# Scores of five batches from unpadded, DMA-transposed q in two bursts a batch, and the tails of two batches in one channel product

## The chip, the cores and the metric

The kernel runs on one core of one Trainium2 chip, as one launch. The metric is its device time in microseconds. The engines are named as the profile names them: PE (TensorE, matmuls) with its weight loads PEld, DVE (VectorE), ACT (ScalarE), POOL (GpSimd) and SP (SyncE), which issues most of the DMAs.

## What is computed

A windowed attention feeds an MLP mixer. Batch 8, 8 heads, 576 positions, head size 64; the model width is 512. Heads 0 to 3 ("plain") see the last 32 positions, heads 4 to 7 ("dilated") every fourth of the last 128. Cut to what matters:

```python
scores = matmul(q, k.transpose(0, 1, 3, 2)) / sqrt(D)        # D = 64
rel = pos[:, None] - pos[None, :]
mask_plain = (rel >= 0) & (rel < 32)                         # heads 0..3
mask_dil = (rel >= 0) & (rel < 128) & (rel % 4 == 0)         # heads 4..7
attn = softmax(where(mask, scores, -1e9))
x = matmul(attn, v)  as  [B, 576, 512]
h = relu(x.T @ w_tok1) @ w_tok2                              # tokens: 576 -> 256 -> 576
u = x + h.T
out = u + relu(u @ w_ch1) @ w_ch2                            # channels: 512 -> 1536 -> 512
```

## The kernel before, in words

All products run in float16 with float32 sums in PSUM. A batch passes through these stages, and the batches overlap: while batch b is in its channel product, batch b+1 passes through values and token mixing, and the scores of b+2 are made.

*Layout.* The 576 positions are four blocks of 128 and a tail of 64. Heads go in pairs, `hp` 0 and 1 plain, 2 and 3 dilated; a pair's 2 x 64 head dimensions fill the 128 partitions. The 512 main positions of a dilated head are held by their remainder modulo 4 (r) and their quotient (m), so that a residue's 128 positions form one dense block under the plain band mask of 32.

*Scores.* `score` (L401) makes one block, transposed, with the keys on the output's partitions: the stationary operand is 128 keys of a pair, both heads' dimensions on the 128 rows, and the moving operand is `qz`, which holds q of one head on its 64 rows and zeros on the other 64. So a matmul contracts over 128 rows, of which half are zeros. `scores_plain` (L415) takes three blocks of 128 keys by 160 queries a head, then in a small bank the fourth block of 160 and the tail of 64; `scores_dil` (L445) takes four residues of 128 by 128 a head, then two tail blocks of 64. ACT takes the exp of each bank (L426, L435, L438, L455, L463) into `attp` and `attd`; in batches 2 and up POOL multiplies these by the band and tail masks (L113 by `mult`). In batches 0 and 1 a further matmul adds a "veil" of large negative numbers instead.

*q and k.* They are loaded, cast by POOL (`c_q`, `c_k`, L103), and turned over: in batches 0 to 2 by PE transposes, from batch 3 on by DMA transposes on SP (`dma_steps`, L346) into `qt`, `kr` (by residue) and `tt` (the tails). `place_steps` (L361) then copies these into `qz` and `kt`: POOL (L371, L373) brings the plain pairs into natural order, DVE (L367, L368, L377, L382) the tails and the dilated pairs.

*Values and mixing.* `values` (L471) multiplies with v; a column of ones gives the sums, and DVE divides (L501, L113). `emit_h1` and `emit_u` are the token mixing. u is turned over by PE (`emit_uT`, L541) up to batch 2 and by DMA from batch 3 on (`uT_dma`, L567; two of its four channel blocks are brought into natural order by ACT into `utd`, `uT_place`, L582).

*Channel product.* `gen_main` (L624) is the long stream: 12 blocks `gp` of four matmuls of 512 columns (L645), each followed by a relu on ACT or DVE (L107, L109); after blocks 5 and 8, `gp_tails` (L632) does the 64 tail columns of this batch, 6 blocks at a time (L636). Then come the token blocks `yp` (L664), 2 x 12 matmuls of 256 columns each, whose result DVE adds to u and SP stores. Two batches, an even and the following odd one, share one token block for their tails (`yp`, L684, in the odd batch).

*The order* is written out by hand: each engine executes its instructions in the order of emission. `interleave` (L693) emits `gen_main`, which says at each step what it costs in microseconds, and a list of side steps, each with a place (the time from the batch's start at which it is due) and a cost; a side step is emitted as soon as the sum of costs reaches its place. "Place 16.2" below means such a due time. It binds no clock; it fixes the order in every engine's queue, SP's included. In batch b from 2 on (L894 and following): values of b+1 from 0.4, casts of b+2 from 2.0, mixing of b+1 from 5.4, DMA transposes of b+2 from 8.5, placements from 13.0 (POOL) and 15.5 (DVE), loads of b+3 from 13.0, scores of b+2 from 16.2 with 2.7 between the pairs (the scores of a pair one spacing later than that), and the placement of u at 29.2.

*PSUM* has eight banks: three `main` (used in rotation by the channel product), two `sc` (rotation) and three `fl` (values and mixing).

## Time and profile before

| | us |
|---|---|
| median of 3 runs | 296.73 (296.33 to 298.97) |
| the profiled execution | 296.67 |
| its span, first to last instruction | 294.9 |
| granted TensorE clock, mean | 0.998 of full speed |
| DMA: moved, mean rate | 52.36 MB, 178 GB/s |

The prediction shows the lines. A line of the timeline has start, duration, engine, line of the kernel, operation, out<-in by the program's names, shape and count; consecutive instructions of a kind are merged (x6), and a bracket gives idle time ahead and what ended it. A PE shape "128\*128 128x160" means 128 rows contracted, 128 stationary columns, 160 moving columns. The recorded duration of a matmul holds its latency and overlaps the next one's. A group of instructions shows count, busy us, mean ns of one, and idle time ahead of them with what ended it.

### The profile page before, as it was taken

What the parts mean: (1) busy time and instruction counts of PE and PEld (TensorE: products, weight loads), DVE (VectorE), ACT (ScalarE), POOL (GpSimd) and SP (SyncE); (2) the same over time, 40 slices, a digit from 0 to 9 for tenths busy, and PEclk for the clock granted to TensorE, in tenths of its full rate; (3) what the DMA queues carried; (4) which work ended last, traced back from release to release, by engine and by line L of the source; (5) the groups of instructions that cost most, each with busy time, mean ns of one, the idle gap of its engine ahead of it and who ended that gap; (6) DMA issues with size and microseconds to landing.
All of it is one profiled execution on the core that took longest, in us unless ns stands there. A gap on an engine that the chain in (4) does not pass through costs nothing.

```text
span 294.9 us, 7473 instructions
## 1 busy us (share of the span) xinstructions
PE 283.1 (96%) x3010; PEld 221.1 (75%) x3010; DVE 153.7 (52%) x326; ACT 132.5 (45%) x259; POOL 181.5 (62%) x246
## 2 busy tenths in 40 slices
PE   5799999999999999999999999999999999999995
PEld 2686679986767977698776977797767977796584
DVE  5775438856738965722744165723753265423122
ACT  2864336376552534356344634365345624323400
POOL 6992056439999899749992999369993920000000
PEclk9999999999999999999999999999999999999999
DMA  7999999987996999699779988499936220421023
GB/s 213 272 213 178 209 322 216 335 189 212 275 190 132 270 288 162 170 210 295 182 106 284 240 216 159 119 293 263 156 66 110 74 71 2 85 81 67 2 71 108
DMA packets 104562, 52.36 MB, mean 178 GB/s; under 512 B 72880, under 2 KB 103472, under 8 KB 104528
## 3 DMA queue, kind: packets, MB, share of 16 engines
q1 hardware_dynamic: 100288, 46.81, 66.9%
q0 software_dynamic: 2640, 3.91, 7.6%
q10 hardware_dynamic: 1600, 1.18, 1.3%
q8 instruction: 23, 0.38, 0.5%
q14 instruction: 11, 0.09, 0.1%
HBM read 37.04 MB, written 9.44 MB: 158 GB/s over the span
## 4 chain that ended last, share of the span: by engine, by line
PE 83%; DMA 6%; POOL 4%; ACT 2%; DVE 2%; SPq 1%; issue 1%; ACTq 0%; POOLq 0%
PE gp L645 27%; PE yp L664 26%; PE gt L636 4%; PE h1p L512 4%; PE up L524 4%; PE sc L406 4%; PE yp L684 4%; DMA w<-in_moe_w_ch_dram 3%; DMA l_q<-in_q_dram 2%; ACT utd L582 1%; PE sm L406 1%; PE av L493 1%; PE h1p L510 1%; PE av L482 1%; PE up L535 1%; DMA l_vt<-in_v_dram 1%
## 5 line engine op out<-in xcount | busy, mean ns | idle before, releaser
L664 PE MATMUL yp<-w,gt 128*128 128x256 f16 x756 | 93.3, 273 | 0.7 <-DVE gt L109 0.7
L664 PEld LDWEIGHTS <-gt 128*128 128x128 f16 x768 | 76.5, 106 | 5.6 <-issue 0.9
L107 ACT ACTIVATE gt<-gp 128x512 f16<-128x512 f32 x69 | 41.2, 597 | 71.4 <-PE gp L645 71.1
L645 PEld LDWEIGHTS <-w 128*128 128x128 f16 x384 | 39.2, 114 | 22.8 <-issue 2.1
L113 POOL TENSOR_TENSOR attp<-attp,const 128x1280 f16<-128x1280 f16 (+1 forms) x24 | 36.4, 1544 | 28.7 <-ACT attp L435 28.5
L674 DVE TENSOR_TENSOR o<-yp,u 128x512 f32<-128x512 f32 x31 | 21.3, 690 | 58.3 <-PE yp L664 55.3
L645 PE MATMUL gp<-utd,w 128*128 128x512 f16 x120 | 45.6, 380 | 0.6 <-ACT utd L582 0.4
L645 PE MATMUL gp<-utm,w 128*128 128x512 f16 x120 | 45.5, 379 | 0.0
L645 PE MATMUL gp<-uT,w 128*128 128x512 f16 x144 | 37.2, 379 | 0.5 <-DMA w<-in_moe_w_ch_dram 0.3
L113 POOL TENSOR_TENSOR attd<-attd,const 128x1024 f16<-128x1024 f16 (+1 forms) x24 | 32.8, 1402 | 0.0
L113 DVE TENSOR_TENSOR xn<-av,rec 128x320 f16<-128x320 f32 x64 | 31.5, 492 | 2.2
L109 DVE TENSOR_SCALAR gt<-gp 128x512 f16<-128x512 f32 x27 | 18.6, 687 | 17.4 <-PE gp L645 16.5
L406 PEld LDWEIGHTS <-kt 128*128 128x128 f16 x272 | 22.4, 101 | 3.5 <-DVE kt L315 1.4
L426 ACT ACTIVATE attp<-sc 128x480 f16<-128x480 f32 x32 | 17.8, 572 | 12.1 <-PE sc L406 12.0
L373 POOL COPY qz<-qt 64x512 f16<-64x512 f16 x20 | 21.6, 1081 | 0.6
L530 DVE TENSOR_TENSOR u<-up,xn 128x512 f16<-128x512 f32 x26 | 17.4, 689 | 8.3 <-PE up L524 8.1
L103 POOL CAST c_q<-l_q 128x512 f16<-128x512 f32 x31 | 19.1, 620 | 4.2 <-DMA l_q<-in_q_dram 4.2
L107 ACT ACTIVATE h<-h1p 128x256 f16<-128x256 f32 x29 | 11.1, 384 | 21.9 <-PE h1p L512 21.9
L103 POOL CAST c_k<-l_k 128x512 f16<-128x512 f32 x29 | 17.9, 620 | 4.2 <-DMA l_k<-in_k_dram 2.8
L455 ACT ACTIVATE attd<-sc 128x512 f16<-128x512 f32 x32 | 18.7, 596 | 4.1 <-PE sc L406 3.6
L501 DVE RECIPROCAL rec<-av 128x5 f32<-128x5 f32 x64 | 12.2, 190 | 13.3 <-PE av L488 6.7
L406 PE MATMUL sc<-qz,kt 128*128 128x160 f16 (+1 forms) x144 | 18.1, 228 | 1.0 <-DVE kt L315 1.0
(138 smaller groups left out, 484.5 us busy)
## 6 DMA issues: line engine op xcount, KB each, us to landing
out_dram<-o SPq DMA_DIRECT2D x72, 128.0 KB, 3.1
l_q<-in_q_dram SPq DMA_DIRECT2D x15, 512.0 KB, 6.1
l_k<-in_k_dram SPq DMA_DIRECT2D x14, 512.0 KB, 5.7
l_vn<-in_v_dram SPq DMA_DIRECT2D x32, 128.0 KB, 5.8
l_vd<-in_v_dram SPq DMA_DIRECT2D x16, 256.0 KB, 4.2
w<-in_moe_w_ch_dram POOLq DMA_DIRECT2D x6, 512.0 KB, 7.7
lt<-in_q_dram SPq DMA_DIRECT2D x8, 128.0 KB, 3.9
l_vt<-in_v_dram SPq DMA_DIRECT2D x8, 128.0 KB, 4.7
```

The costliest lines, as they stand in the source:

```text
L103: eng.tensor_copy(out=out, in_=in_)
L107: nc.scalar.activation(out=out, in_=in_, func=AF.Relu)
L109: eng.tensor_scalar_max(out=out, in0=in_, scalar1=0.0)
L113: eng.tensor_tensor(out=out, in0=x, in1=y, op=ALU.mult)
L373: nc.gpsimd.tensor_copy(out=natural(qz[hp][halves[h], h, 0:512]), in_=qta[halves[h], hp].rearrange("p r m -> p m r"))
L406: nc.tensor.matmul(out=out, lhsT=lhsT, rhs=qz[hp][:, h, queries], start=hide is None, stop=True)
L426: nc.scalar.activation(out=blocks[:, h, 0:3, 0:BLK], in_=p[:, 0:3 * BLK].rearrange("p (b c) -> p b c", c=BLK), func=AF.Exp, scale=0.125)
L455: nc.scalar.activation(out=a[:, h, 0:DTL], in_=p, func=AF.Exp, scale=0.125)
L530: nc.vector.tensor_tensor(out=u16(b, s), in0=blocks4(p), in1=blocks4(xn[b][:, s]), op=ALU.add)
L645: nc.tensor.matmul(out=p, lhsT=w3_block(cb, mb), rhs=uT[(b, cb)][0], start=(i == 0), stop=(i == 3))
L664: nc.tensor.matmul(out=p[:, c], lhsT=gta[:, mb, a0:m0 + 512:4] if half else gta[:, mb, a0:a0 + 128], rhs=w4[mb][:, c], start=(mb == 0), st ...
L674: nc.vector.tensor_tensor(out=blocks4(o32), in0=blocks4(p), in1=u16(b, s), op=ALU.add)
```

## The change

1. **Scores of batches 3 to 7** come from a new function, `scores_twin`, called twice a batch (g = 0 plain, g = 1 dilated). Each block is made by two matmuls, one for each head of the pair, that contract over 64 rows: partitions 0 to 63 for the first head, 64 to 127 for the second, each head with its own PSUM bank. q is read straight from `qt` and `tt`. Plain queries come in residue order, and the exp writes them in natural order, with a step of four elements. A burst holds six banks (two `sc`, three `fl`, one `main`). All its matmuls are emitted together, then all its exps and masks.
2. **Placements** of q go. `place_steps` keeps the copies of k, all on POOL: the two plain pairs, the tails, and the last 128 positions of the dilated pairs.
3. **Attention tails** of all heads move to one tile, `attt` [128, 4, 2, 320], two blocks of 64 a head. The plain heads' fourth block shrinks from 160 to 128 queries, and its last 64 queries become a tail block of their own, in all batches. One mask multiplication serves the tails of two pairs in `scores_twin`.
4. **Tails of the channel product**: `gp_tails` runs in odd batches alone, over 128 columns (the even batch's 64 and its own), 4 blocks at a time after blocks 3, 6 and 9. Even batches turn no tail of u over, by PE or by DMA.
5. **Relus**: from batch 1 on DVE takes blocks 1 and 5 of 12 (before 1, 5 and 9); the tails' relus go to DVE once and ACT twice.
6. **Order**: bursts at 16.4 and 20.8 in even batches, 18.8 and 23.2 in odd ones (25.2 and 29.4 in batch 1); placements from 12.0; loads of b+3 from 17.6; u's placement at 22.4 (even) or 24.8 (odd) for two of its blocks and 2.6 later for the other two; in batch 0 most steps 1.4 earlier. Some fixed tiles and memsets differ accordingly.

The diff, cut to its core:

```diff
         for a in attp:
             nc.gpsimd.memset(
-                a[:, :, 0:PTL].rearrange("p h (b c) -> p h b c", c=PST)[:, :, :, BLK:PST], 0.0)
-            nc.gpsimd.memset(a[:, :, PTL:PW], 1.0)
-        for a in attd:
-            nc.vector.memset(a[:, :, DTL:DW], 1.0)
+                a.rearrange("p h (b c) -> p h b c", c=PST)[:, :, :, 128:PST], 0.0)
+        nc.vector.memset(attt, 1.0)
...
     def place_steps(b):
 
-        halves = [slice(0, 64), slice(64, 128)]
-
         def tails():
-            for h in range(2):
-                nc.vector.tensor_copy(out=qza[halves[h], :, h, 512:S], in_=tta[halves[h], :, 0:64])
-            nc.vector.tensor_copy(out=kta[:, :, 512:S], in_=tta[:, :, 64:128])
+            nc.gpsimd.tensor_copy(out=kta[:, :, 512:S], in_=tta[:, :, 64:128])
 
         def plain(hp):
             nc.gpsimd.tensor_copy(out=natural(kt[hp][:, 0:512]), in_=kra[:, hp].rearrange("p r m -> p m r"))
-            for h in range(2):
-                nc.gpsimd.tensor_copy(out=natural(qz[hp][halves[h], h, 0:512]),
-                                      in_=qta[halves[h], hp].rearrange("p r m -> p m r"))
-
-        def dil(h):
-            nc.vector.tensor_copy(out=qza[halves[h], 2:4, h, 0:512],
-                                  in_=qta[halves[h], 2:4].rearrange("p a r m -> p a (r m)"))
-
-        def dil_k():
-            for hp in (2, 3):
-                nc.vector.tensor_copy(out=natural(kt[hp][:, 384:512]),
-                                      in_=kra[:, hp, :, 96:128].rearrange("p r m -> p m r"))
-
-        return ([lambda hp=hp: plain(hp) for hp in range(2)],
-                [tails] + [lambda h=h: dil(h) for h in range(2)] + [dil_k])
+
+        def dil(hp):
+            nc.gpsimd.tensor_copy(out=natural(kt[hp][:, 384:512]),
+                                  in_=kra[:, hp, :, 96:128].rearrange("p r m -> p m r"))
+
+        return [lambda: plain(0), tails, lambda: plain(1), lambda: dil(2), lambda: dil(3)]
...
         p = small_bank(b, hp)
         for h in range(2):
-            score(b, hp, h, p[:, BLK * h:BLK * h + BLK], slice(384, 512), slice(384, 384 + BLK), wide)
-        for h in range(2):
-            score(b, hp, h, p[:, 320 + 64 * h:384 + 64 * h], slice(512, 640), slice(512, S), narrow)
+            score(b, hp, h, p[:, 128 * h:128 * h + 128], slice(384, 512), slice(384, 512),
+                  veil[:, 0:128] if veils else None)
+        tail_scores(b, hp, p, 256)
         nc.scalar.activation(
-            out=blocks[:, :, 3, 0:BLK], in_=p[:, 0:320].rearrange("p (h c) -> p h c", c=BLK),
+            out=blocks[:, :, 3, 0:128], in_=p[:, 0:256].rearrange("p (h c) -> p h c", c=128),
             func=AF.Exp, scale=0.125)
-        nc.scalar.activation(
-            out=tl, in_=p[:, 320:448].rearrange("p (h c) -> p h c", c=64), func=AF.Exp, scale=0.125)
+        tail_exp(hp, p[:, 256:512])
         if not veils:
             mult(nc.gpsimd, blocks[:, :, :, 0:BLK], blocks[:, :, :, 0:BLK], band)
-            mult(nc.gpsimd, tl, tl, band[:, 0, :, 0:64])
+            mult(nc.gpsimd, tail_cols(hp), tail_cols(hp), tails_seen[0])
         yield 0.21
...
+    def scores_twin(b, g):
+
+        tags = (("sc", 2), ("sc", 2), ("fl", 3), ("fl", 3), ("fl", 3), ("main", 3))
+        ps = [bank(*tags[i], f"sc_{b}_{g}_{i}") for i in range(6)]
+        small = ps[4:6]
+
+        def twin(hp, banks, c, keys, queries):
+            for h in range(2):
+                rows = slice(64 * h, 64 * h + 64)
+                n = c.stop - c.start
+                nc.tensor.matmul(out=banks[h][:, c], lhsT=keys(rows), rhs=queries(rows), start=True, stop=True)
+
+        for j in range(2):
+            hp = 2 * g + j
+            if g == 0:
+                for kb in range(3):
+                    twin(hp, ps[2 * j:2 * j + 2], slice(BLK * kb, BLK * kb + BLK),
+                         lambda rows: kt[hp][rows, 128 * kb:128 * kb + 128],
+                         lambda rows: qta[rows, hp, :, 32 * kb:32 * kb + 40])
+            else:
+                for r in range(4):
+                    twin(hp, ps[2 * j:2 * j + 2], slice(128 * r, 128 * r + 128),
+                         lambda rows: kra[rows, hp, r], lambda rows: qta[rows, hp, r])
+        for j in range(2):
+            hp = 2 * g + j
+            if g == 0:
+                twin(hp, small, slice(256 + 128 * j, 384 + 128 * j),
+                     lambda rows: kt[hp][rows, 384:512], lambda rows: qta[rows, hp, :, 96:128])
+            for x in range(2):
+                twin(hp, small, slice(128 * j + 64 * x, 128 * j + 64 * x + 64),
+                     lambda rows: kt[hp][rows, 384 + 128 * x:512 + 128 * x], lambda rows: tta[rows, hp, 0:64])
+        yield 0.87
+
+        def exp(out, in_):
+            nc.scalar.activation(out=out, in_=in_, func=AF.Exp, scale=0.125)
+
+        def main(hp):
+            for h in range(2):
+                p = ps[2 * (hp % 2) + h]
+                if g == 0:
+                    exp(plain_blocks(hp)[:, h, 0:3, 0:BLK].rearrange("p b (m r) -> p b r m", r=4),
+                        p[:, 0:3 * BLK].rearrange("p (b r m) -> p b r m", r=4, m=40))
+                else:
+                    exp(attd[hp - 2][:, h], p)
+
+        def rest():
+            for h in range(2):
+                p = small[h]
+                if g == 0:
+                    for hp in range(2):
+                        exp(plain_blocks(hp)[:, h, 3, 0:128].rearrange("p (m r) -> p r m", r=4),
+                            p[:, 256 + 128 * hp:384 + 128 * hp].rearrange("p (r m) -> p r m", r=4))
+                t = attt[:, 2 * g:2 * g + 2, h, 64:TW].rearrange("p a (x c) -> p a x c", c=128)[:, :, :, 0:64]
+                exp(t, p[:, 0:256].rearrange("p (a x c) -> p a x c", x=2, c=64))
+
+        def mask(hp):
+            if g == 0:
+                w = plain_blocks(hp)[:, :, :, 0:BLK]
+                mult(nc.gpsimd, w, w, band)
+            else:
+                w = attd[hp - 2].rearrange("p h (r c) -> p h r c", c=128)
+                mult(nc.gpsimd, w, w, band[:, :, :, 0:128])
+
+        main(2 * g)
+        if g:
+            mask(2)
+        main(2 * g + 1)
+        if g:
+            mask(3)
+        rest()
+        if not g:
+            mask(0)
+        t = attt[:, 2 * g:2 * g + 2].rearrange("p a h c -> p (a h) c")[:, :, 64:TW].rearrange(
+            "p z (x c) -> p z x c", c=128)[:, :, :, 0:64]
+        mult(nc.gpsimd, t, t, tails_seen[g])
+        if not g:
+            mask(1)
+        yield 0.0
...
+        c0 = 0 if odd else 64
+        nc.tensor.matmul(out=av[:, 4], lhsT=attt[:, hp, i, c0:c0 + 128],
+                         rhs=va[:, 3, h, :] if hp < 2 else vt[b % 2][:, h - 4, :], start=True, stop=False)
+        nc.tensor.matmul(out=av[:, 4], lhsT=attt[:, hp, i, c0 + 128:c0 + 256], rhs=va[:, 4, h, :],
+                         start=False, stop=True)
...
+        if by_dma(b):
+            for g in range(2):
+                for i, f in enumerate([scores_twin(b, g)] * 2):
+                    steps.append((t0 + g * dt, 0.86 * (i == 0), lambda f=f: next(f)))
+            return steps
...
-            for t, tail in ((2.0, True), (6.0, False)):
+            for t, tail in ((2.0, True), (6.0, False))[1 - b % 2:]:
                 steps.append((t_u + t * du, 0.0, lambda tail=tail: uT_dma(b, tail)))
-            for i, cb in enumerate(CBS):
-                steps.append((t_uT + 0.5 * i, 0.0, lambda cb=cb: uT_place(b, cb)))
+            for t, cb in ((0.0, 2), (0.0, 0), (2.6, 3), (2.6, 1)):
...
-        def gp_tails(half):
-            p = bank("main", 3, f"gt_{b}_{half}")
-            for i in range(6):
+        def gp_tails(g):
+            p = bank("main", 3, f"gt_{b}_{g}")
+            for i in range(4):
                 for cb in order:
                     nc.tensor.matmul(
-                        out=p[:, 64 * i:64 * i + 64], lhsT=w3_block(cb, 6 * half + i), rhs=uT[(b, cb)][1],
+                        out=p[:, 128 * i:128 * i + 128], lhsT=w3_block(cb, 4 * g + i), rhs=uT[(b, cb)][1],
                         start=(cb == order[0]), stop=(cb == order[-1]))
-            relu(nc.scalar if half else nc.vector, gta[:, 6 * half:6 * half + 6, t0:t0 + 64],
-                 p[:, 0:384].rearrange("p (i t) -> p i t", t=64))
+            relu(nc.scalar if g else nc.vector, gta[:, 4 * g:4 * g + 4, 512:640],
+                 p.rearrange("p (i t) -> p i t", t=128))
 
         for mb in range(NMB):
...
-            relu(nc.vector if mb % (2 if b == 0 else 4) == 1 else nc.scalar, gta[:, mb, m0:m0 + 512], p)
+            relu(nc.vector if (mb % 2 == 1 if b == 0 else mb in (1, 5)) else nc.scalar, gta[:, mb, m0:m0 + 512], p)
             yield 0.43
-            if mb in (5, 8):
-                gp_tails(int(mb == 8))
-                yield 0.7
+            if odd and mb in (3, 6, 9):
+                gp_tails(mb // 3 - 1)
+                yield 0.9
...
-            steps += score_steps(3, 22.2, 2.8) + at(9.0, 0.6, cast_steps(3))
+            steps += score_steps(3, 25.2, 4.2) + at(9.0, 0.6, cast_steps(3))
...
+            late = 2.4 * (b % 2)
             if b + 1 < B:
-                steps += value_steps(b + 1, 0.4, 0.95) + mix_steps(b + 1, 5.4, 9.0, 11.4, 29.2)
+                steps += value_steps(b + 1, 0.4, 0.95) + mix_steps(b + 1, 5.4, 9.0, 11.4, 22.4 + late)
             if b + 2 < B:
-                steps += at(2.0, 0.6, cast_steps(b + 2)) + score_steps(b + 2, 16.2, 2.7)
-                steps += at(8.5, 0.7, dma_steps(b + 2)) + at(13.0, 0.4, place_steps(b + 2)[0])
-                steps += [(t, 0.0, f) for t, f in zip((15.5, 19.2, 20.0, 20.8), place_steps(b + 2)[1])]
+                steps += at(2.0, 0.6, cast_steps(b + 2)) + score_steps(b + 2, 16.4 + late, 4.4)
+                steps += at(8.5, 0.7, dma_steps(b + 2)) + at(12.0, 0.4, place_steps(b + 2))
             if b + 3 < B:
-                steps += at(13.0, 0.9, load_steps(b + 3))
+                steps += at(17.6, 0.9, load_steps(b + 3))
         interleave(gen_main(b), steps)
```

120 lines of the change are left out of this document (57 added, 63 removed).

## The prediction

> **What bounds the kernel now.** I read the page's engine table and chain first, then the table of stretches, then TensorE's timeline matmul by matmul.
>
> ```profile
> PE 283.1 (96%) x3010; PEld 221.1 (75%) x3010; DVE 153.7 (52%) x326; ACT 132.5 (45%) x259; POOL 181.5 (62%) x246
> ...
> PE 83%; DMA 6%; POOL 4%; ACT 2%; DVE 2%; SPq 1%; issue 1%; ACTq 0%; POOLq 0%
> ```
>
> PE is busy for 96% of the span, and 83% of the chain that ended last lies on it. A busy PE is not yet a full PE, so the next view takes two batches of the steady part (columns: length, then busy time and count by engine):
>
> ```profile
> 138.00:171.90 33.90, 33.60 (x344) 25.74 (x344) 16.27 (x37) 16.82 (x32) 28.47 (x33) 1.00 0.91 218
> 171.90:204.00 32.10, 31.92 (x342) 25.24 (x341) 16.10 (x37) 15.24 (x30) 24.63 (x31) 1.00 0.82 200
> ```
>
> PE is without work for 0.30 and 0.18 us there, at a granted clock of 1.00; ACT and DVE are busy about half of the time. So a change is worth what it takes from PE's stream of matmuls, plus or minus the stalls that it removes or makes. The price of a matmul in the stream is not its duration but the distance to the next start:
>
> ```profile
> 158.44 0.58 PE L406 MATMUL sc<-qz,kt 128*128 128x160 f16 x6
> 158.86 1.03 PE L684 MATMUL yp<-w,gt 128*128 128x512 f16 x4
> 159.72 0.36 PE L406 MATMUL sm<-qz,kt 128*128 128x160 f16 x4
> ...
> 160.57 0.37 PE L406 MATMUL sc<-qz,kt 128*128 128x160 f16 x3
> 160.78 0.82 PE L664 MATMUL yp<-w,gt 128*128 128x256 f16 x6
> 161.43 0.37 PE L406 MATMUL sc<-qz,kt 128*128 128x160 f16 x3
> ...
> 162.30 0.36 PE L406 MATMUL sm<-qz,kt 128*128 128x160 f16 x4
> 162.49 0.82 PE L664 MATMUL yp<-w,gt 128*128 128x256 f16 x6
> 163.15 0.39 PE L406 MATMUL sc<-qz,kr 128*128 128x128 f16 x4
> 163.37 0.82 PE L664 MATMUL yp<-w,gt 128*128 128x256 f16 x6
> ...
> 165.56 0.28 PE L406 MATMUL sm<-qz,kt 128*128 128x64 f16 x4
> 165.68 0.39 PE L406 MATMUL sc<-qz,kr 128*128 128x128 f16 x4
> ```
>
> Six score matmuls of 160 columns take 158.86 - 158.44 = 0.42 us, 70 ns each; four of 128 take 0.22, 55 each; four of 64 take 0.12, 30 each; the group of two 160s and two 64s takes 0.19; six of 256 (160.78 to 161.43) take 0.65, 109 each; four of 512 (158.86 to 159.72) take 0.86, 215 each. A 64-column matmul is recorded as 0.28 - 3 x 0.03 = 0.19 us long, so about 0.16 us of it is latency that the stream hides.
>
> **The change part by part, in PE's stream.** *Scores of batches 3 to 7.* Today a batch has, for each of four plain heads, 3 x 70 + half of 0.19 us, and for each of four dilated heads 4 x 55 + 2 x 30 ns: 4 x 305 + 4 x 280 = 2.34 us. Every one contracts over 128 rows, of which 64 are zeros. The two heads of a pair now go as two 64-row matmuls on the two halves of the partitions, into two PSUM banks. No matmul of this trace has fewer than 128 rows, so the price of a pair is unknown. Lower bound: the halves overlap entirely and a pair costs one matmul, 2 x (3 x 70 + 55 + 2 x 30) + 2 x (4 x 55 + 2 x 30) = 1.21 us a batch, a gain of 1.13. Upper bound: no overlap, 4 x 325 + 4 x 280 = 2.42, a loss of 0.08. Between them I take overlap of the streams, but two weight loads after one another: the shortest slot that holds a weight load and its matmul is 30 ns, so a pair costs at least 60. Then it is 2 x (3 x 70 + 3 x 60) + 2 x 6 x 60 = 1.50 us, a gain of 0.84 a batch, 4.2 in five batches (bounds +0.4 to -5.7).
>
> A second unknown is what it costs to pass from 128-row to 64-row matmuls and back: two passages for each of ten bursts. At least nothing; at most the 0.16 us of latency that the stream otherwise hides, 3.2 us over 20 passages. I take 0.10 each, nearer to the latency, since weights of the new shape must replace those of the old: +2.0.
>
> The latency row is the one to weigh against a rule. The Trainium skill (TensorEngine Tiling (Array Packing), Key Properties) says that changing the tiling mode, not just the tile, drains TensorE, and also that different tiles load weights and multiply in parallel. By the first sentence the passages would cost the whole 3.2 us and the forecast would be 292.5; by the second, pairs would cost 1.21 us and the forecast, with my passages, would be 289.8. No run here shows either yet.
>
> *Tails in the channel product.* Each batch streams 48 matmuls of 64 columns against the channel weights:
>
> ```profile
> 146.56 0.96 PE L636 MATMUL gt<-utt,w 128*128 128x64 f16 x24
> 147.36 0.38 PE L645 MATMUL gp<-utd,w 128*128 128x512 f16 x1
> ```
>
> 24 take 0.80 us, so a pair of batches pays 96 x 33.3 = 3.20 us. Afterwards the odd batch alone streams 48 of 128 columns, at 55 ns 2.64 us. Four pairs: -2.2. Were a 128-column matmul against these strided weights dearer by the 3 ns that a 64-column one is (33 for 30), it would be -1.7.
>
> *Small things on PE.* The even batches 0 and 2 lose four transposes of 128 columns each (8 x 55 ns = -0.44; batch 0's four stand before a wait for weights and may bring nothing). In batches 0 to 2 a plain head's 160 + 64 columns become 128 + 64 + 64, +15 ns a head, doubled where a veil is added: 4 x 15 x (2 + 2 + 1) = +0.3. Together -0.1.
>
> **Stalls that go.** Three spots in the steady part have a next start later than the stream allows:
>
> ```profile
> 121.95 2.32 PE L645 MATMUL gp<-uT,w 128*128 128x512 f16 x10
> 124.94 1.47 PE L664 MATMUL yp<-w,gt 128*128 128x256 f16 x12 [0.67 <-DVE gt L109]
> ```
> and in the chain, in order of time:
>
> ```profile
> 122.16 0.69 DVE u L530
> 122.85 0.97 DVE qz L367
> ```
>
> back in TensorE's timeline, two batch boundaries:
>
> ```profile
> 136.50 1.48 PE L664 MATMUL yp<-w,gt 128*128 128x256 f16 x12
> 138.17 0.38 PE L645 MATMUL gp<-utd,w 128*128 128x512 f16 x1 [0.20 <-ACT utd L582]
> ...
> 138.84 0.19 PE L488 MATMUL av<-vv,attp 128*128 128x65 f16 x1
> 139.16 0.38 PE L645 MATMUL gp<-utd,w 128*128 128x512 f16 x1
> ```
> ```profile
> 201.85 1.48 PE L664 MATMUL yp<-w,gt 128*128 128x256 f16 x12
> 203.51 0.38 PE L645 MATMUL gp<-utd,w 128*128 128x512 f16 x1 [0.18 <-ACT utd L582]
> ```
>
> At 121.95 ten matmuls need 2.15 us and the next starts after 2.99: 0.84 lost, because the relu of block 9 stands on DVE behind DVE's placement of q's tails (L367). That placement goes, and block 9's relu moves to ACT. At 136.50 twelve need 1.31 and the next starts after 1.67 (0.36 lost); then 0.32 instead of 0.03 at 138.84 (0.29); at 201.85, 0.35, and I count the same 0.29 behind it. All four wait for the two `utd` copies on ACT, which stand behind the last exps at the end of the batch. They move from place 29.2 to 22.4 (24.8 in odd batches) of the written order, behind the second burst. Sum: -2.1.
>
> **What the bursts bring to ACT.** The exps of a burst stand together in ACT's queue, and for the plain pairs they write with a step of four elements. First ACT's timeline, then the groups of instructions kept apart by shape (count, busy us, mean ns, idle before):
>
> ```profile
> 158.91 1.03 ACT L426 ACTIVATE attp<-sc 128x480 f16<-128x480 f32 x2 [1.50 <-PE sc L406]
> ...
> 160.51 0.27 ACT L438 ACTIVATE attp<-sm 128x128 f16<-128x128 f32 x1
> ```
> ```profile
> L107 ACT ACTIVATE gt<-gp 128x512 f16<-128x512 f32 x69 | 41.2, 597 | 71.4 <-PE gp L645 71.1
> ...
> L426 ACT ACTIVATE attp<-sc 128x480 f16<-128x480 f32 x32 | 17.8, 572 | 12.1 <-PE sc L406 12.0
> ...
> L582 ACT COPY utd<-utm 128x512 f16<-128x512 f16 x10 | 10.4, 1087 | 2.3 <-DMA utm<-u 2.3
> ...
> L463 ACT ACTIVATE attd<-sm 128x256 f16<-128x256 f32 x16 | 6.2, 384 | 8.5 <-PE sm L406 8.5
> ```
>
> Two wide exps back to back take 1.03 for 2 x 0.57, so each holds ACT 0.46 and hides 0.1 of its length. A plain burst is then 4 x 0.46 + 4 x 0.17 + 2 x 0.28 = 3.1 us of ACT, from 0.5 us after PE's first score (158.44 to 158.91). No strided write of ACT is in the trace. Low end: nothing, the 0.57 of L426. High end: L582, which reads SBUF in steps of 256 bytes, 1.09. The nearest row by step is on POOL, which reads in steps of eight bytes in L763 and of 256 in L371:
>
> ```profile
> L371 POOL COPY kt<-kr 128x512 f16<-128x512 f16 x10 | 10.8, 1081 | 0.3
> ...
> L763 POOL COPY w2p<-w 128x512 f16<-128x512 f16 x2 | 1.2, 656 | 0.1
> ```
>
> Eight bytes cost POOL almost nothing (0.66 against 1.08), so I take 0.57. The Trainium skill (SBUF — State Buffer, SBUF: two separate sides) wants two accesses on a 16-byte line for full bandwidth, which steps of eight bytes keep; these POOL rows agree, and by that rule the exps cost 0.57 too.
>
> Walking the written order: in even batches the burst follows the last relu, and nothing on PE needs ACT for 4.7 us (0.8 burst, six half blocks of 0.65); ACT is done after 4.2. In odd batches (3 and 5) the burst lies between the halves of channel block 11, so its relu queues behind all ten exps: it ends at 0.5 + 3.1 + 0.6 = 4.2 us after the burst's start (4.3 with the signal), while PE asks for it after 0.8 + 0.1 + 0.43 + 11 x 0.215 = 3.7. That is a new stall of 0.6 each, +1.2. At batch 1 the burst is behind all channel relus. What is late next at the batch boundaries is the DMA that turns u over: the copies have waited 2.3 us for it in all ten (L582); it is issued at place 17.4, which leaves them 5 places.
>
> **Edits costed at nothing.** A batch's four half copies of q on POOL (1.08 us each) and all its placements on DVE go; the copy of k's tails and two short copies of k come to POOL from DVE. POOL has room:
>
> ```profile
> L113 POOL TENSOR_TENSOR attp<-attp,const 128x1280 f16<-128x1280 f16 x12 | 31.7, 2643 | 28.7 <-ACT attp L435 28.5
> ...
> L113 POOL TENSOR_TENSOR attd<-attd,const 128x1024 f16<-128x1024 f16 x12 | 25.6, 2130 | 0.0
> ```
>
> It sits 28.5 us waiting for exps. Its masks start one burst later than now, though, and in even batches end some 3 us into the next one (2 x 2.64 + 2 x 2.13 + tails of about 1.1 a burst from 20 us on); the first dilated head wants them at 4.6, so 1.5 us of cover is left; without it PE waits the excess in each even batch. On SP, loads move from place 13.0 to 17.6, behind the transposes of u; their casts stand in the next batch, so cover is several us. The longer DVE memset at the start lies before q's and k's first transposes, which wait for the constants.
>
> **Sum** against the profiled run's 296.67 us (span 294.9 and 1.8 around it; the median is 296.73): -4.2 + 2.0 - 2.2 - 0.1 - 2.1 + 1.2 = -5.4, which gives 291.3.
>
> **The rivals.** *Free packing* (0.15): pairs at one matmul and no price for a passage: -5.7 - 2.2 - 0.1 - 2.1 + 1.2 = -8.9, 287.8. For it: weight loads are busy in 75% of the span and still never end a wait. Against: each score pair needs two of them in 55 ns. *The halves don't overlap*, so the packing does not do what it says (0.20): +0.4 + 3.2 - 2.2 - 0.1 - 2.1 + 1.2 = +0.4, 297.1. For it: nothing in the trace shows two matmuls side by side. *ACT becomes the bound of the burst* (0.17), the slow side: at L582's price a wide exp holds ACT 0.92, a short one 0.3, a plain burst 5.5 us. Odd batches then wait for the relu 2.8 us each; in batches 1, 2 and 4 the second burst finds the bank of the first's small scores in use for about 1.3 us each; POOL's masks come 2.3 later and overrun their cover by 0.8 in two batches. That is 5.6 + 3.9 + 1.6 = 11.1 in place of 1.2, 301.2. It decides from about 0.8 us for a 480-column exp. Against it: the eight-byte row.
>
> **How the numbers follow.** My forecast, 291.3, has 0.45 and a range of its own of 289.3 to 293.7 (passages at nothing; passages at 3.2 and the new stalls twice as long). The remaining 0.03 is for masks or loads that come late on their own. About 1% is what a measurement of this kernel can tell from no change: 293.8 and 299.7. Faster: 0.43 of the forecast's 0.45, and the 0.15; same: the 0.20, and 0.05 from the edges of the forecast and the remainder; slower: the 0.17. The range reaches over free packing and no overlap and stops short of the ACT case: 287.5 to 299.0.
>
> **What would show it.** Right: pairs of 160 columns starting every 70 to 75 ns, of 64 every 60; a gap of about 0.1 us at each burst's ends; a wide strided exp of 0.57; in batches 3 and 5 a wait of 0.6 for the relu ahead of the tail's token block; no gap at the batch boundaries before `utd`; 24 tails in no even batch. Wrong: pairs at 110 or 140 ns, exps over 0.8, PE waiting for a score bank or for masks.

## The result and the profile after

The changed kernel takes 307.43 us (median of 4 runs, 306.52 to 308.78), against 296.53 us for the kernel before on the same chip: a ratio of 1.034, 95% interval 1.029 to 1.039. The forecast was 291.3 with a range of 287.5 to 299.0. It was wrong, and on the wrong side. One of the five executions of experiment 8, 364.85 us at a mean granted clock of 0.75, was in a slower state; it is left out of that experiment's ratio, and the median given there, 292.32 us, is 292.22 without it. Lines in this part are those of the changed kernel: L499 holds the exps of the bursts, L475 their matmuls, L106 relu on ACT, L717 and L708 the channel product and its tails, L756 the token product of the tails, L736 the rest of it.

The engine table and the chain of the page come first:

```profile
PE 284.1 (93%) x2850; PEld 216.6 (71%) x2850; DVE 132.4 (43%) x279; ACT 148.5 (48%) x276; POOL 165.8 (54%) x227
...
PE 75%; ACT 10%; DMA 7%; POOL 3%; issue 2%; DVE 1%; SPq 1%; ACTq 0%; POOLq 0%
```

TensorE has 160 matmuls fewer, yet it is the chain's engine for 75% where it was 83, and ACT has gone from 2% to 10%. The next view cuts the span at the first channel matmul of each batch (columns: window, length, busy us and count of PE, PEld, DVE, ACT and POOL, granted clock, DMA share, GB/s). Batches 0 to 5 of the kernel before:

```profile
27.21:68.74 41.53, 40.14 (x480) 33.10 (x478) 23.88 (x49) 20.86 (x44) 17.54 (x31) 1.00 0.97 242
68.74:105.95 37.21, 37.04 (x411) 29.12 (x409) 26.32 (x47) 18.64 (x39) 35.20 (x43) 1.00 0.96 227
105.95:138.17 32.22, 31.36 (x336) 24.72 (x335) 16.47 (x37) 14.77 (x30) 26.67 (x33) 1.00 1.02 213
138.17:172.14 33.97, 33.84 (x346) 25.98 (x346) 16.11 (x37) 16.65 (x31) 28.54 (x33) 1.00 0.91 219
172.14:203.51 31.37, 31.19 (x336) 24.73 (x335) 15.61 (x37) 14.75 (x30) 23.90 (x31) 1.00 0.81 198
203.51:237.49 33.98, 33.85 (x346) 25.97 (x346) 16.11 (x37) 16.65 (x31) 28.55 (x33) 1.00 0.56 117
```

and of the changed kernel:

```profile
27.61:70.38 42.77, 39.60 (x444) 31.51 (x441) 23.30 (x48) 20.07 (x42) 16.06 (x28) 1.00 0.97 251
70.38:110.81 40.43, 38.20 (x411) 29.05 (x409) 17.68 (x39) 22.45 (x44) 32.81 (x42) 1.00 0.83 219
110.81:141.00 30.19, 29.14 (x292) 22.11 (x291) 12.72 (x27) 17.90 (x32) 22.48 (x29) 1.00 0.71 163
141.00:180.28 39.28, 35.91 (x353) 26.80 (x352) 14.01 (x29) 19.19 (x34) 29.77 (x36) 0.96 0.95 202
180.28:210.45 30.17, 29.13 (x293) 22.10 (x292) 12.72 (x27) 17.88 (x32) 16.61 (x23) 1.00 0.69 176
210.45:249.56 39.11, 35.73 (x353) 26.77 (x352) 14.01 (x29) 19.20 (x34) 27.57 (x31) 0.96 0.59 125
```

Batches 2 and 4 are 2.0 and 1.2 us shorter, batches 3 and 5 are 5.3 and 5.1 longer, and batches 0 and 1 are 1.2 and 3.2 longer. Some of this is meant: from an even batch 48 tail matmuls of 64 columns go (1.6 us), and the odd one after it pays 48 of 128 columns for them (1.1 us more than its own 48 of 64). In batch 3 TensorE is without work for 39.28 - 35.91 = 3.4 us, and the clock column, which read 1.00 everywhere, says 0.96. Batches 3 and 5 have one place where it all stands, here batch 3 in TensorE's timeline:

```profile
160.37 0.65 PE L475 MATMUL sc<-qt,kt 64*128 64x160 f16 x14
...
161.58 2.75 PE L756 MATMUL yp<-w,gt 128*128 128x512 f16 x12
167.42 0.82 PE L736 MATMUL yp<-w,gt 128*128 128x256 f16 x6 [3.08 <-ACT gt L106]
```

and in ACT's:

```profile
160.85 5.00 ACT L499 ACTIVATE attp<-sc 128x480 f16<-128x480 f32 x6 [0.20 <-PE sc L475]
165.57 0.48 ACT L499 ACTIVATE attt<-sc 128x256 f16<-128x256 f32 x1
165.94 0.74 ACT L499 ACTIVATE attp<-sc 128x128 f16<-128x128 f32 x2
166.39 0.49 ACT L499 ACTIVATE attt<-sc 128x256 f16<-128x256 f32 x1
166.76 0.61 ACT L106 ACTIVATE gt<-gp 128x512 f16<-128x512 f32 x1
```

The last twelve matmuls start between 161.58 and 163.96 (11 x 0.216 later), then the next one starts at 167.42 instead of 0.216 later: 3.25 us lost. It waits for the relu of block 11, and that relu stands on ACT behind ten exps that take from 160.85 to 166.8. This is the wait that the forecast had put at 0.6. The groups by shape say why:

```profile
L499 ACT ACTIVATE attp<-sc 128x480 f16<-128x480 f32 x20 | 22.3, 1315 | 0.4 <-PE sc L475 0.4
...
L428 ACT ACTIVATE attp<-sc 128x480 f16<-128x480 f32 x12 | 6.7, 577 | 4.1 <-PE sc L392 4.0
```

The same 480 columns take 577 ns where they are written in a run (L428, batches 0 to 2) and 1315 where they are written with a step of four (L499). In the even batches the same exps hold up something else, the bank of the small scores; TensorE's timeline in batch 2:

```profile
132.27 0.71 PE L475 MATMUL sc<-qt,kr 64*128 64x128 f16 x16
133.39 0.19 PE L475 MATMUL sc<-tt,kt 64*128 64x64 f16 x1 [0.40 <-ACT attt L499]
134.22 0.27 PE L475 MATMUL sc<-tt,kt 64*128 64x64 f16 x7 [0.65 <-ACT attt L499]
```

Sixteen 128-column halves, 56 ns a pair, need 0.45 us, so the first small score of the second burst could start at 132.72. It starts at 133.39, and the next at 134.22: 0.67 and 0.80 us lost, each waiting for the exp that empties a bank of the first burst. Last, the clock, in windows laid along the stretch in which it was low:

```profile
161.57:164.99 3.42, 2.76 (x13) 1.18 (x12) 0.62 (x1) 3.42 (x4) 0.00 (x0) 1.00 0.88 183
164.99:168.40 3.41, 0.98 (x14) 0.72 (x15) 0.07 (x1) 2.38 (x8) 1.86 (x1) 1.00 1.00 307
168.40:171.81 3.41, 3.41 (x35) 2.57 (x30) 0.00 (x0) 3.12 (x7) 3.41 (x3) 0.50 1.08 367
233.26:236.67 3.41, 0.51 (x3) 0.11 (x2) 0.69 (x1) 3.41 (x9) 0.69 (x1) 1.00 0.27 59
236.67:240.08 3.41, 3.22 (x34) 2.28 (x34) 0.00 (x0) 1.29 (x4) 3.41 (x3) 0.50 0.09 18
```

For 3.41 us behind each of the two long waits the granted clock is 0.50; half of that, about 1.7 us, is lost on top of each wait. The two stretches start 236.67 - 168.40 = 68.27 us apart, 20 times 3.413. The Trainium skill (TensorE: Matmul & The Clock Gate, What's actually happening) gives the gate a window of 3413 ns that runs freely; this trace agrees in length and spacing.

### The profile page after: what moved, and what is told of

It is laid out like the page before. It is cut to its first block, busy times and chain, and to the rows that moved or that the text cites. A ratio compares the mean times of both kernels' runs of the same rounds, so it can differ in the third digit from the quotient of the medians.

```text
span 307.0 us, 7094 instructions
## 1 busy us (share of the span) xinstructions
PE 284.1 (93%) x2850; PEld 216.6 (71%) x2850; DVE 132.4 (43%) x279; ACT 148.5 (48%) x276; POOL 165.8 (54%) x227
## 4 chain that ended last, share of the span: by engine, by line
PE 75%; ACT 10%; DMA 7%; POOL 3%; issue 2%; DVE 1%; SPq 1%; ACTq 0%; POOLq 0%
PE gp L717 23%; PE yp L736 23%; ACT attp L499 7%; PE h1p L579 5%; PE up L591 3%; PE gt L708 3%; DMA l_k<-in_k_dram 3%; PE sc L475 2%; DMA const<-consts 2%; PE yp L756 2%; DMA l_q<-in_q_dram 2%; PE sc L392 1%; PE h1p L577 1%; PE sc L390 1%; PE av L560 1%
## 5 line engine op out<-in xcount | busy, mean ns | idle before, releaser
L736 PE MATMUL yp<-w,gt 128*128 128x256 f16 x756 | 88.8, 277 | 6.2 <-ACT gt L106 6.2
L736 PEld LDWEIGHTS <-gt 128*128 128x128 f16 x768 | 79.3, 107 | 13.7 <-issue 7.0
L106 ACT ACTIVATE gt<-gp 128x512 f16<-128x512 f32 x76 | 45.4, 597 | 89.3 <-PE gp L717 89.0
L112 POOL TENSOR_TENSOR attp<-attp,const 128x1280 f16<-128x1280 f16 x12 | 31.3, 2611 | 49.1 <-ACT attp L499 43.3
L717 PEld LDWEIGHTS <-w 128*128 128x128 f16 x384 | 39.8, 114 | 23.4 <-issue 1.6
L717 PE MATMUL gp<-utd,w 128*128 128x512 f16 x120 | 45.6, 380 | 0.0
L717 PE MATMUL gp<-utm,w 128*128 128x512 f16 x120 | 45.5, 379 | 0.0
L717 PE MATMUL gp<-uT,w 128*128 128x512 f16 x144 | 36.3, 379 | 0.7 <-ACT uT L100 0.7
L499 ACT ACTIVATE attp<-sc 128x480 f16<-128x480 f32 (+1 forms) x40 | 28.8, 920 | 0.4 <-PE sc L475 0.4
L112 POOL TENSOR_TENSOR attd<-attd,const 128x1024 f16<-128x1024 f16 x12 | 25.3, 2125 | 0.0
L106 ACT ACTIVATE h<-h1p 128x256 f16<-128x256 f32 x29 | 11.1, 383 | 16.5 <-PE h1p L579 16.4
L108 DVE TENSOR_SCALAR gt<-gp 128x512 f16<-128x512 f32 x20 | 13.8, 688 | 11.7 <-PE gp L717 11.3
L392 PEld LDWEIGHTS <-kt 128*128 128x128 f16 x144 | 12.1, 105 | 3.6 <-DVE kt L314 1.9
L112 POOL TENSOR_TENSOR attt<-attt,const 128x512 f16<-128x512 f16 (+1 forms) x14 | 14.2, 1014 | 0.0
L606 DVE TENSOR_TENSOR u16t<-up,xn 64x512 f16<-64x512 f32 x7 | 4.8, 689 | 19.8 <-PE up L602 19.8
L708 PEld LDWEIGHTS <-w 128*128 128x128 f16 x192 | 11.9, 113 | 1.6
```

The costliest lines, as they stand in the source:

```text
L106: nc.scalar.activation(out=out, in_=in_, func=AF.Relu)
L108: eng.tensor_scalar_max(out=out, in0=in_, scalar1=0.0)
L112: eng.tensor_tensor(out=out, in0=x, in1=y, op=ALU.mult)
L392: nc.tensor.matmul(out=out, lhsT=lhsT, rhs=qz[hp][:, h, queries], start=hide is None, stop=True)
L499: nc.scalar.activation(out=out, in_=in_, func=AF.Exp, scale=0.125)
L708: nc.tensor.matmul(out=p[:, 128 * i:128 * i + 128], lhsT=w3_block(cb, 4 * g + i), rhs=uT[(b, cb)][1], start=(cb == order[0]), stop=(cb == ...
```

## The experiments

The theory that the profile suggests, called A: the strided write of the exps is what the change loses by, through ACT's queue, and the 64-row scores themselves bring their gain. The rivals put the loss into something else that the change brings: the 64-row bursts, the places of the written order, or loads. Numbers 1 to 4 ran on one chip, beside the kernel before (296.42 us).

**1. Write in a run.** The exp reads the PSUM bank with the step and writes the keys' columns in natural order; in the wide exps

```
-  exp(plain_blocks(hp)[:, h, 0:3, 0:BLK].rearrange("p b (m r) -> p b r m", r=4),
-      p[:, 0:3 * BLK].rearrange("p (b r m) -> p b r m", r=4, m=40))
+  exp(plain_blocks(hp)[:, h, 0:3, 0:BLK].rearrange("p b (m r) -> p b m r", r=4),
+      p[:, 0:3 * BLK].rearrange("p (b r m) -> p b m r", r=4, m=40))
```

and the short ones of 128 likewise.

> The plain exps write in natural order without a step and read the bank in steps of 40 columns instead; nothing else changes. Theory A (a strided write makes ACT's exp slow, 1.32 us for 480 columns, and so makes ACT the bound of a burst): the exp falls to about 0.6 us, the two waits of 3.25 us for the relu in batches 3 and 5 fall to 0.6 each, the half-clock stretches of 3.4 us behind them (1.7 each) go, and the waits for the small scores' bank (1.4, 1.4, 1.9) go: 307.4 - 5.3 - 3.4 - 4.7 = 294.0. Rival B (the relu's place behind the exps costs the time whatever an exp costs): the waits stay above 2 us, 304 or more. Rival C (64-row matmuls and the passages to them cost the time): no change, 307.

Measured: 294.06 us, ratio 0.992 (0.990 to 0.994), 13.4 us less than the changed kernel: A. The wide exps:

```profile
L499 ACT ACTIVATE attp<-sc 128x480 f16<-128x480 f32 x20 | 9.8, 579 | 0.4 <-PE sc L475 0.4
```

the wait for block 11's relu in batch 3:

```profile
157.05 2.75 PE L756 MATMUL yp<-w,gt 128*128 128x512 f16 x12
160.05 0.81 PE L736 MATMUL yp<-w,gt 128*128 128x256 f16 x6 [0.25 <-ACT gt L106]
```

and batches 2 and 3 by window:

```profile
107.77:136.48 28.71, 28.71 (x293) 21.98 (x291) 12.73 (x27) 15.12 (x32) 22.67 (x29) 1.00 0.73 159
136.48:171.30 34.82, 34.28 (x353) 25.91 (x351) 14.01 (x29) 16.38 (x34) 26.96 (x32) 1.00 0.98 232
```

Reading PSUM in steps of 160 bytes costs ACT nothing (579 against 577), writing SBUF in steps of eight bytes costs 1315. The bank waits are gone (batch 2 is busy throughout), the wait for block 11's relu is down from 3.25 to 160.05 - 157.05 - 12 x 0.216 = 0.41 us, and the clock stays at 1.00. This one edit gives back more than the whole loss.

**2. Relu first.** The burst of odd batches moves behind block 11's relu in the written order; the strided write stays.

```
-            late = 2.4 * (b % 2)
+            late = 2.8 * (b % 2)
```

> The changed kernel with its slow exps, but in odd batches the burst is due 0.4 later, behind the relu of channel block 11. Theory A: the waits for the relu go, and batches 3 and 5 wait for the bank of the small scores instead, as batches 2 and 4 do, 1.4 each: 307.4 - 2 x (3.25 + 1.7 - 1.4) = 300.3. Rival B: nothing is left to wait for, 307.4 - 9.9 = 297.5 or less. Rival C: 307.

Measured: 301.29 us, ratio 1.016 (1.014 to 1.019), 1.0 above A's 300.3. The long wait and its half clock are gone, and odd batches now wait where the even ones do, in batch 3:

```profile
163.99 0.72 PE L475 MATMUL sc<-qt,kr 64*128 64x128 f16 x16
165.10 0.19 PE L475 MATMUL sc<-tt,kt 64*128 64x64 f16 x1 [0.40 <-ACT attt L499]
165.93 0.27 PE L475 MATMUL sc<-tt,kt 64*128 64x64 f16 x7 [0.65 <-ACT attt L499]
```

So 6.1 of the 13.4 us came from the relu's place in ACT's queue and the clock behind it, net of the new waits of 0.66 + 0.80 us in each odd batch. The rest needs the exps themselves to be short.

**3. Both, and 4. both with batch 0's steps at the places of the kernel before.** The second adds

```
-  ((12.6, 14.8), (14.0, 16.8), (16.2, 18.6), (17.6, 20.2))
+  ((14.0, 16.2), (15.4, 18.2), (17.6, 20.0), (19.0, 21.6))
-  value_steps(1, 20.3, 0.7)
+  value_steps(1, 21.7, 0.7)
-  mix_steps(1, 24.2, 27.0, 29.0, 34.8, 1.1)
+  mix_steps(1, 25.6, 28.4, 30.4, 36.2, 1.1)
```

> Both edits: natural-order writes, and the relu of block 11 ahead of the burst. Theory A: 294.0 less the 0.6 each that is left in batches 3 and 5, 292.8. Rival B: as the relu-first kernel alone, so no gain from the exps, 297 to 300. Rival C: 307 less a little.

> As with both edits, and the steps of batch 0 back at the places of the kernel before (14.0, 20.0, 21.7, 25.6 and so on instead of 1.4 earlier). In the changed kernel PE waits 0.70, 0.56 and 0.32 us in batch 0 for casts of batch 1 that wait for loads. If the earlier places cause that: 1.0 to 1.6 less than with both edits alone, about 291.5. If it is the loads that come later whatever PE does: the same time as with both edits alone.

Measured: 294.08 us, 0.992 (0.989 to 0.995), and 293.41 us, 0.989 (0.987 to 0.991). The first missed its forecast of 292.8: its odd batches are 0.4 us shorter than those of experiment 1, as expected, but its profiled run starts later:

```profile
19.26 0.93 PE L854 MATMUL w_p<-w1p,spread 128*128 128x256 f16 x7 [1.71 <-DMA w1p<-in_moe_w_tok_dram]
```

That wait for the first weights differs between runs of nearly the same start and hides a gain of 0.8 in the profiled run; that it did so in the others isn't shown. The places of batch 0 moved nothing in the time that two intervals can tell apart. In the profiles they did move something: batch 1 takes 37.73 us for 38.74 in number 3, and batch 0 41.97 for 41.13.

**5. Halves apart.** (Numbers 5 to 8: the kernel before took 296.79 us on their chip; 9 and 10: 296.57.) On the base of number 4, each burst does all matmuls of the lower 64 rows, then all of the upper.

```
-            for h in range(2):
+            for h in (half,):
                 rows = slice(64 * h, 64 * h + 64)
...
+        for half in range(2):
             for j in range(2):
                 hp = 2 * g + j
```

> Base: natural-order writes, relu first, batch 0 as before (293.4 us, span 291.7). In each burst of batches 3 to 7 all matmuls of the lower 64 rows come first, then all of the upper 64 rows; nothing else changes. Theory A (the gain of the 64-row scores comes from two neighbours that run side by side on the two halves): a 160-column matmul then starts every 69 ns, one of 128 every 56, one of 64 every 28, each alone; the bursts cost one whole copy more, 2 x (3 x 69 + 56 + 2 x 28) + 2 x (4 x 56 + 2 x 28) = 1.20 us a batch, 6.0 in five batches: 299.4 us. Rival B (a matmul of 64 rows takes half of the time of one with 128 whatever stands beside it, or TensorE's queue finds the partner further down): the starts stay at 35 and 28 ns on the mean and the time at 293.4, within 0.5.

Measured: 297.64 us, ratio 1.003 (1.001 to 1.005). Against the base's 0.989 that is 0.0139 x 296.6 = 4.1 us. Batch 2 is 29.68 us long for 28.70, and its first burst reads

```profile
124.40 0.64 PE L475 MATMUL sc<-qt,kt 64*128 64x160 f16 x7
124.88 0.22 PE L475 MATMUL sc<-tt,kt 64*128 64x64 f16 x2
124.92 0.24 PE L475 MATMUL sc<-qt,kt 64*128 64x160 f16 x2
...
125.02 0.19 PE L475 MATMUL sc<-tt,kt 64*128 64x64 f16 x1
125.06 0.49 PE L475 MATMUL sc<-qt,kt 64*128 64x160 f16 x5
```

The first seven take 124.88 - 124.40 = 0.48 us, 69 ns each (six of 160 and one of 128), where the packed burst does fourteen in the same time. So the gain is overlap of neighbours, as A says. But the lower half's last small scores (sc<-tt,kt) and the upper half's first 160s mix at 124.92 to 125.06: by their starts, TensorE found partners a few matmuls further down. In batches 2 to 5 the edit cost 0.97 or 0.98 us a batch, not 1.20, and in batch 1 0.74: 4.7 by the lengths of the batches, where A said 6.0. The 4.1 of the medians holds the differing starts of the runs as well.

**6. Passages.** Matmuls of 128 rows between the twins of a burst's first pair of heads:

```
+        def cut(j, hp):
+            if j == 0:
+                nc.tensor.matmul(out=ps[2][:, 0:64], lhsT=kt[hp][:, 0:128], rhs=kt[hp][:, 0:64], start=True, stop=True)
```

> Same base. Into each burst go three matmuls of 128 rows and 64 columns (their result is overwritten by the scores that follow), between twins of the first pair of heads: 30 in five batches. Theory A (each change of shape costs about 0.09 us, on entering and on leaving): each inserted matmul costs 0.03 of its own and two passages, 0.03 + 2 x 0.09 = 0.21, 30 of them 6.3 us: 299.7. Rival B (the gap at the burst's ends comes from something else that stands there, such as the first wait for a bank or the weights of another tile, and a change of shape is free): 30 x 0.03 = 0.9, 294.3.

Measured: 300.37 us, ratio 1.011 (1.008 to 1.014), 0.0216 x 296.6 = 6.4 us above the base: A. One insertion after another:

```profile
131.08 0.23 PE L475 MATMUL sc<-qt,kr 64*128 64x128 f16 x2
131.24 0.20 PE L479 MATMUL sc<-kt 128*128 128x64 f16 x1
131.38 0.23 PE L475 MATMUL sc<-qt,kr 64*128 64x128 f16 x2
```

A round takes 131.38 - 131.08 = 0.30 us. Take away 0.056 for the pair of 128 columns and 0.03 for the inserted matmul, and 0.21 is left for two passages: 0.11 each. What TensorE does in that time isn't shown.

**7. Steps of two and of eight.** On the base of number 4, the wide exps of the first pair write in steps of two elements (r=2), those of the second in steps of eight (r=8), on two lines of their own (L507 and L511). The keys' columns no longer fit the mask and the values, so this kernel does not compute the attention:

```
+  w = plain_blocks(hp)[:, h, 0:3, 0:BLK]
+  if hp == 0:
+      nc.scalar.activation(
+          out=w.rearrange("p b (m r) -> p b r m", r=2), in_=p[:, 0:3 * BLK].rearrange("p (b r m) -> p b r m", r=2, m=80),
...
+  else:
+      nc.scalar.activation(
+          out=w.rearrange("p b (m r) -> p b r m", r=8), in_=p[:, 0:3 * BLK].rearrange("p (b r m) -> p b r m", r=8, m=20),
```

> Same base, but the wide exps of the first plain pair write in steps of two elements (4 bytes) and those of the second in steps of eight (16 bytes), both reading PSUM in one run; the keys' columns are so permuted against the mask and the values, and the output is not the attention that is asked for. Theory A (ACT pays about 1.5 ns more per element as soon as its 2-byte elements are not neighbours, whatever the step): both take about 1.32 us, as step four did. Rival B (what counts is how many elements fall on a stretch of 16 bytes: eight in a run, four at step two, two at step four, one at step eight): step two takes 0.58 to 0.9, step eight 1.8 to 2.6 us. Time: with A about that of relu first alone without its strided short exps, 299 to 301; with B step two costs nothing and step eight 2 x 0.5 to 2 x 1.3 more than 1.32, 296 to 302, so the verdict rests on the two rows.

```profile
L511 ACT ACTIVATE attp<-sc 128x480 f16<-128x480 f32 x10 | 22.3, 2506 | 0.0
...
L507 ACT ACTIVATE attp<-sc 128x480 f16<-128x480 f32 x10 | 6.3, 703 | 0.0
```

B by its figures: 579 ns in a run, 703 at step two, 1315 at step four, 2506 at step eight. From step two on, doubling the step doubles the time or nearly so. B's reason, the count of elements on 16 bytes, isn't told apart from a price that grows with the step's length, and step two, with four elements on 16 bytes, already costs 124 ns. The time of the whole, 307.96 us in a single run, lies above what either theory gave: with 2.5 us exps the second burst waits longer for its banks, and two stretches at half clock appear, the first of them here, the second from 203.95 on:

```profile
132.27:135.68 3.41, 1.83 (x31) 1.36 (x28) 0.00 (x0) 3.41 (x10) 1.32 (x1) 1.00 0.86 218
135.68:139.09 3.41, 3.41 (x18) 2.47 (x17) 0.69 (x1) 3.41 (x6) 3.41 (x3) 0.50 1.10 376
166.40:169.81 3.41, 2.27 (x30) 1.58 (x29) 0.69 (x1) 3.41 (x8) 0.00 (x0) 1.00 0.99 266
169.81:173.22 3.41, 2.98 (x33) 2.73 (x32) 0.69 (x1) 3.41 (x9) 3.27 (x2) 1.00 1.05 362
```

The waits of batches 2 and 3 are equal, but one falls into one window of 3.41 us (TensorE busy for 1.83 of it, then half clock) and the other across two (2.27 busy, then full clock). The second stretch stands behind a window with 1.86 busy.

**8. The tail's relu on ACT.** What is left in number 4's odd batches is a wait of 0.45 us in each, where DVE's relu of the first four tails stands ahead of the normalisation of a value head.

```
-            relu(nc.scalar if g else nc.vector, gta[:, 4 * g:4 * g + 4, 512:640],
+            relu(nc.scalar, gta[:, 4 * g:4 * g + 4, 512:640],
```

> Same base, with the relu of the first four tails of an odd batch on ACT in place of DVE, where it stood ahead of the normalisation of a value head. Theory A (the stalls of 0.45 us at 143.2 and 206.4 come from that place on DVE): both go, 293.4 - 0.9 = 292.5 us, lengths of the odd batches 34.0. Rival B (they come from the row of PSUM banks or from ACT's relu of h, the releaser that the trace names): the stalls stay or grow, 293.4 to 294.

Measured: 292.32 us, ratio 0.984 (0.981 to 0.987), the best of all, 1.6% below the kernel before. The odd batches are 34.23 us long, against 34.42 in number 4 and the 34.0 expected, so only 0.2 of each 0.45 went, and what makes the other 0.25 stays open. The profiled runs differ by another 0.4 ahead of batch 0, which the edit does not touch.

**9. Two idles.** On the base of number 8, with the bursts back ahead of the relu, one exp is repeated to lengthen the wait for it:

```
+        if not g:
+            for _ in range({5: 5, 7: 7}.get(b, 0)):
+                exp(...)
...
-            late = 2.8 * (b % 2)
+            late = 2.4 * (b % 2)
```

> Base: the version with the tail's relu on ACT (292.3 us, span 290.9), with the burst of the odd batches back at its place of the changed kernel, ahead of block 11's relu; the first wide exp of the plain burst is repeated on ACT, five times in batch 3 and seven times in batch 5, with the same result each time. TensorE is so made to wait for the relu, about 0.4 + 5 x 0.46 = 2.7 us in batch 3 and 0.4 + 7 x 0.46 = 3.6 in batch 5. Theory A (the half clock that the changed kernel showed for 3.4 us behind each of its idles of 3.1 to 3.3 us follows from the length of the idle, at about 3 us): a half-clock stretch of 3.4 us, worth 1.7, stands behind the second idle alone: 292.3 + 2.7 + 3.6 + 1.7 = 300.3. Rival B (an idle costs its own length, and the half clock came from something else that these stretches held, such as the two bursts or the transfers): no stretch at half clock, 298.6. Rival C (any idle of some microseconds brings it): two stretches, 302.0.

Measured: 304.13 us, ratio 1.026 (1.022 to 1.030). By the idles, a repeated exp held ACT for (3.28 - 0.41) / 5 = 0.57 us and not 0.46, so the idles became 3.3 and 4.5 us, and the run does not hold the short idle that it was made for:

```profile
161.08:164.49 3.41, 1.19 (x22) 0.93 (x23) 0.00 (x0) 2.17 (x8) 2.03 (x1) 1.00 1.01 313
164.49:167.90 3.41, 3.41 (x31) 2.45 (x25) 0.00 (x0) 3.36 (x7) 3.41 (x3) 0.50 1.08 372
225.93:229.34 3.41, 2.07 (x10) 0.85 (x9) 0.69 (x1) 3.22 (x7) 0.00 (x0) 1.00 0.36 80
229.34:232.75 3.41, 0.42 (x4) 0.38 (x4) 0.00 (x0) 2.94 (x10) 1.27 (x1) 1.00 0.35 77
232.75:236.16 3.41, 3.41 (x36) 2.42 (x34) 0.00 (x0) 2.14 (x5) 3.41 (x3) 0.50 0.00 0
```

B falls: experiment 1, with the same bursts and exps written in a run, stays at 1.00, and the longer idle alone brings half clock back. 292.3 + 3.3 + 4.5 + 2 x 1.7 = 303.5 is close to what was measured. A and C aren't told apart by this run. The rows of number 7 speak against both, since waits of about 2 us brought half clock in one batch and not in the next, and point to windows: around these waits, half clock follows a window of 3.41 us in which TensorE is busy for 0.42 to 1.86 us, and doesn't follow one with 2.07 (225.93) or more. Busy time alone is not the whole rule, though: in number 7 the window from 16.21 to 19.63, ahead of batch 0, holds 1.85 us, and the next one is at 1.00. The Trainium skill (TensorE: Matmul & The Clock Gate, What's actually happening) speaks of an idle window; here one that is a little more than half busy by the records can still bring half clock.

**10. Batch 0 later.** On the base of number 8:

```
-            steps += mix_steps(1, 25.6, 28.4, 30.4, 36.2, 1.1)
+            steps += mix_steps(1, 25.6, 29.1, 31.2, 37.0, 1.1)
```

> Base: the same version; in batch 0 the second half of h1, the rows of u and its transposes stand 0.7 to 0.8 later in the written order. Theory A (batch 0 still loses about 1.9 us more to waits than the kernel before, since its stream is 1.6 us shorter without the tails while the written places are the same, so that the work for batch 1 asks for its inputs too early): the waits of 0.47 and 0.46 us at 60.1 and 62.2 shrink, and batch 0 takes 0.5 to 1.0 us less: 291.3 to 291.8. Rival B (the waits belong to copies and loads that are late by themselves, and move with the steps): the time stays at 292.3, within 0.5.

Measured: 293.56 us, ratio 0.988 (0.986 to 0.991), no gain. In its profile batch 0 takes 43.0 us for 42.0 and batch 1 0.35 less: waits stand at the later steps too, and the two longest are now 0.72 and 0.77 us. My theory of these waits falls.

## Why the prediction was wrong

The step that failed is the price of the strided exp: "Eight bytes cost POOL almost nothing (0.66 against 1.08), so I take 0.57." It is 1.315 us, above the high end of 1.09 as well. The bound came from copies on POOL and a copy on ACT that read with a step; here the step is in the write, and ACT's read of PSUM with a step (experiment 1) is free. A row of another engine, of the other direction, bounded nothing. The rule that I set beside it failed with it: the Trainium skill (SBUF — State Buffer, SBUF: two separate sides) asks for two accesses on a 16-byte line for full bandwidth. Step four keeps two and takes 2.3 times as long, step two keeps four and takes 1.2 times. For this write the measurement decides.

Point by point against the sum:

- *Scores, -4.2.* Better than forecast. Pairs cost one matmul, the lower bound: 69 ns for 160 columns, 56 for 128, 28 for 64, so about 1.2 us a batch and a gain of 5 x 1.13 = 5.7. The step that a pair costs "at least 60", for two weight loads, was wrong too.
- *Passages, +2.0.* Right in size: 0.10 us at a burst's ends, 0.11 in experiment 6, which ties the gap to the change of shape. The 0.10 was a choice between bounds of 0 and 0.16, so that it came out is partly luck, and the reason given for it, the weights of the new shape, isn't shown.
- *Channel tails, -2.2.* Right: twelve of 128 columns take 0.67 us, 56 ns each, so 4 x (3.20 - 48 x 0.056) = -2.0.
- *Stalls that go, -2.1.* Right: with short exps TensorE is busy for 28.71 of 28.71 us in batch 2, and no wait for `utd` is left, in the changed kernel as in experiment 1.
- *New stalls, +1.2.* Here the loss is. Odd batches: 2 x 3.25 for block 11's relu, and 2 x 1.7 for the half clock, which no step had. Second bursts: about 1.5 us each in batches 2 and 4, and in batch 1, which waits at the same place, 40.43 - 38.76 = 1.7 by its length in experiment 1. With exps at 0.58 the forecast's 0.6 was 0.41.
- *Not in the sum.* In each odd batch TensorE waits 0.45 us at DVE's relu of four tails at once; 0.2 of it went with that relu (number 8). And batches 0 and 1 lost some 3 us to waits even with short exps: batch 0 should be 48 x 0.033 = 1.6 shorter and is 0.4 longer in experiment 1, batch 1 should be about 0.35 longer (1.08 for the pair's tails less 0.73 for scores) and is 1.55 longer. In the changed kernel part of it stands at 40.8 to 43.7 us, where TensorE waits for casts that wait for q's and k's loads. Batch 1's part came from the places of batch 0's steps: with those of the kernel before (number 4) it is 37.73 us, within 0.2 of what was expected. Batch 0's 2.0 us stay open: it is 41.97 us long in number 4 and 43.0 with later places (number 10).

So the rival on the slow side, *ACT becomes the bound of the burst*, was the right one in place and order: relu in odd batches, the bank of the small scores in the others, from "about 0.8 us for a 480-column exp". Its 301.2 was worked out at 1.09, and left out the clock; POOL's masks, which it also charged, showed no wait in batches 2 to 5. That the row it turns on was missing was known ("No strided write of ACT is in the trace"), and still I gave the case only 0.17.

Without the step in the write, the change is what it was meant to be: 294.06 us, and 292.32 with the bursts behind the relu and the tails' relu on ACT. That is still above 291.3, by less than the 2.0 us that batch 0 loses.

## What to carry to other kernels

When a layout needs a permutation between PSUM and SBUF, put the step into the read of the PSUM bank and not into the write: the same exp took 579 ns the one way and 1315 the other. Before costing a strided access, ask for a row of the same engine and the same direction; without one the range has to reach past the dearest row, and the chance with it. Two products over 64 rows are worth packing if they stand side by side and many of them follow one another, since a change of shape costs as much as a pair and a half of 160 columns; and a wait of TensorE of 2 us or more can cost up to 1.7 us more than itself.
